# Fused attention and gated feed-forward on one core: value products re-cut by head group, VectorE's score blocks from the first unit into the last

## The chip, the cores and the metric

One core of one Trainium2 chip. The metric is the device time of one execution in microseconds (us), and every kernel is run several times. The profile of one of these executions covers the span from the first to the last instruction, which is about 1.7 us shorter than the time. Beside each run stands the mean clock that TensorE was granted (1.0 is full speed). All runs here are of the same state by the rule used for them (none over 1.5% above the fastest of its kernel), so they are compared as they are; but inside that state time and granted clock move together, and this turns out to matter.

PE is TensorE, PEld its weight loads, DVE is VectorE, ACT is ScalarE, SP is SyncE.

## The reference, cut to what matters

```python
# x: 2048 x 512, 32 heads of 16, F = 1792, all bf16
g = sigmoid((x * gate_w).sum(-1, keepdims=True))
q, k, v = split(x @ wqkv)                       # 32 heads
p = softmax(q @ k.T / 4)                        # per head, 2048 x 2048
a = (p @ v).reshape(S, D) @ wo
b = (silu(x @ w_gate) * (x @ w_up)) @ w_down
return g * a + (1 - g) * b
```

The costly part is the exponential: 32 heads of 2048 x 2048 scores. In the kernel before, ScalarE takes them from TensorE's accumulators in 882 instructions (821.9 us busy) and VectorE in 284 evictions of a block (195.2 us).

## The kernel before

The work is cut into 32 units: four heads (a "group") times one quarter of the queries. The first four units take group 0 for the four quarters; the others follow quarter by quarter. A unit has 16 key tiles times 4 heads: 64 score blocks of 128 x 512. A planner at build time decides, block by block, who takes the exponential.

ScalarE takes blocks in pairs, VectorE takes four blocks as one group with a polynomial in three 16-bit passes each of two kinds:

```python
def emit_pair(bs):                     # ScalarE: two blocks, one instruction
    s_t = ps_s.tile([P, 2 * QBW], F32, tag="s", name="s_t")
    ...                                # two score matmuls into s_t
    act(out=e_t[:], in_=s_t[:], func=ACT.Exp, scale=inv_sqrt_dh)

def emit_d(b):                         # VectorE: one block into the one bank "d"
    d_t = ps_d.tile([P, QBW], F32, tag="d", name="d_t")
    score(d_t[:, :], b)
    ...
    # evicts d_t into y; after the fourth block of the group six passes over 2048 elements:
    # z<-y, u<-z, u<-u*u, u<-u*z, y<-y+u, y<-y, and then the group's value products may run
```

Which of the two it is, is decided here. `un` is the unit, `at_` the block in it. A new VectorE group may begin only while `at_` is at most 50 in an ordinary unit, at most 4 in the last, and not at all in unit 0:

```python
def to_vector():
    un, at_ = divmod(nxt, 4 * KT)
    if vcur:
        ...                            # a group already begun is completed
    if not un or at_ > (50 if un < UNITS - 1 else 4) or y_live[0] >= 3 or sum(v[0] for v in vops) > 6:
        return 0
    return 1
```

A VectorE group that comes after its unit's accumulator (`o_ps`) has been closed is late: its value products go into a separate bank `x_ps`, and VectorE then needs two operations, a copy of the closed bank (`of<-o_ps`) and a sum (`osb<-of,x_ps`). A group that is in time needs only one cast (`osb<-o_ps`).

```python
def pv(bs, last):
    extra = un < closed                # the unit's bank is closed: a late group
    if extra:
        o = m_tile("x_ps")
    ...
    if extra:
        def add():
            vec.tensor_tensor(out=(of_of if blocks[un] else osbs)[un][:, :], in0=of_of[un][:, :], in1=o[:, :], op=ALU.add)
```

The head: keys and queries of group 0 are projected, `|k|` is reduced to a bound that is added to the queries, and four key tiles' values for all 32 heads are evicted by ScalarE before the first exponential:

```python
act(out=q0r[:, :], in_=qp0[:, :], func=ACT.Copy)
for i in range(2):
    vec.tensor_reduce(out=kpart0[:, i:i + 1], in_=kp0[i][:, :], axis=AX.X, op=ALU.max, apply_absolute_value=True)
    v_now(i)                           # four 512-column matmuls, one ScalarE eviction
    act(out=kaug[:, 0, i * 2 * QBW:(i + 1) * 2 * QBW], in_=kp0[i][:, :], func=ACT.Identity, ...)
    ...
vec.scalar_tensor_tensor(out=kneg0, ...)
v_now(2)
mm(bp0[:, :], lhsT=kneg0, rhs=aq0[:, :], start=True, stop=True)      # the bound
...
v_now(3)
```

And the end, after the last unit's sum `osb`. First the projection of the unit before (`al`, `a_l`, four matmuls), then the denominators (`dt`), their reciprocals, the normalised heads, the projection again and the stores:

```python
last_mm(0, osbs[un - 1])                              # al, al, a_l, a_l
for tq in range(TQ):
    mm(dt[:, 4 * tq:4 * tq + 4], lhsT=osb[:, tq * P:(tq + 1) * P], rhs=sel_t[:, :], start=True, stop=True)
recip16(rt[:, :], dt[:, 0:4 * TQ])
...
last_mm(1, on_l)
```

## Time and profile before

| | |
|---|---|
| time, median of the three runs known when predicting | 874.49 us (873.94 to 876.53) |
| span of the profiled execution, mean granted clock | 872.4 us, 0.997 |
| exponentials on ScalarE, VectorE groups | 882, 71 |
| first exponential starts, last one ends | 19.27, 863.62 |
| ScalarE idle among the exponentials | 4.8 us |

The three stretches to keep apart are the head (up to the first exponential, 19.27 us), the stream of exponentials (844.35 us), and the tail (from the end of the last exponential to the end of the span, 8.8 us). ScalarE's time in the stream is a count of instructions times 0.92 us (a run of 58 exponentials took 53.47 us), plus its gaps. The lines are shown in the prediction.

### The profile page before, as it was taken

The numbers are of one execution on the slowest core, as the hardware profiler recorded it, in microseconds if no ns is written. First come the engines' busy times: TensorE is split into PE (matmuls) and PEld (weight loads), VectorE is DVE, ScalarE is ACT, GpSimd is POOL, SyncE is SP. The second block draws the span as 40 slices with busy tenths as digits, with TensorE's granted clock in tenths as the row PEclk, the third lists the DMA queues.
The fourth block names the chain that finished last, engine by engine and source line by source line (L and its number), as shares of the span: only waits on it lengthen the run. The fifth ranks groups of instructions, "written<-read, shape, count | busy, mean of one in ns | idle before, by whom it ended". The sixth has DMA issues, their size and how long they took to land.

```text
span 872.4 us, 14196 instructions
## 1 busy us (share of the span) xinstructions
PE 784.8 (90%) x5078; PEld 207.6 (24%) x5168; DVE 786.9 (90%) x1103; ACT 845.4 (97%) x947; POOL 7.1 (1%) x29
## 2 busy tenths in 40 slices
PE   6999999999999899999989888899898989989985
PEld 2222222222222222222222222222222222222221
DVE  6379999999999999999999999999999998999984
ACT  3999999999999999999999999999999999999995
POOL 3000000000000000000000000000000000000000
PEclk9999999999999999999999999999999999999999
DMA  8401121031101112210011121110011121000000
GB/s 208 111 1 28 29 50 38 21 69 28 31 11 26 40 33 73 52 37 11 4 31 31 34 55 45 42 28 4 4 25 36 36 57 48 21 10 4 5 20 24
DMA packets 87535, 31.98 MB, mean 37 GB/s; under 512 B 75120, under 2 KB 87016, under 8 KB 87464
## 3 DMA queue, kind: packets, MB, share of 16 engines
q1 hardware_dynamic: 86408, 30.94, 14.5%
q8 instruction: 40, 0.66, 0.3%
q10 hardware_dynamic: 1056, 0.13, 0.1%
q14 instruction: 31, 0.25, 0.1%
HBM read 20.83 MB, written 2.34 MB: 27 GB/s over the span
## 4 chain that ended last, share of the span: by engine, by line
ACT 42%; PE 34%; DVE 11%; issue 11%; SPq 1%; DMA 0%; ACTq 0%; DVEq 0%
ACT e_t L161 38%; PE s_t L158 13%; PE o_ps L158 7%; DVE y_t L167 5%; PE d_t L158 4%; PE dps L158 3%; ACT th L161 3%; DVE u_t L167 2%; PE gp L158 2%; PE qp L158 1%; PE up L158 1%; SPq L174 1%; PE kp L158 1%; DVE mt L167 1%; PE a_ps L158 1%
## 5 line engine op out<-in xcount | busy, mean ns | idle before, releaser
L161 ACT ACTIVATE e_t<-s_t 128x1024 bf16<-128x1024 f32 x882 | 821.9, 1079 | 4.8 <-PE s_t L158 3.7
L158 PE MATMUL s_t<-qx,kaug 64*128 64x512 bf16 x1656 | 330.1, 384 | 52.8 <-ACT e_t L161 49.5
L167 DVE TENSOR_SCALAR y_t<-d_t 128x512 uint16<-128x512 f32 x284 | 195.2, 687 | 29.7 <-PE d_t L158 26.2
L158 PEld LDWEIGHTS <-kaug 64*128 64x128 bf16 x2048 | 100.0, 93 | 379.4 <-issue 376.3
L158 PE MATMUL o_ps<-e_t,vaug 128*32 128x512 bf16 x1764 | 172.8, 387 | 1.3 <-ACT e_t L161 0.7
L158 PE MATMUL d_t<-qx,kaug 64*128 64x512 bf16 x264 | 99.6, 377 | 0.6 <-DVE y_t L167 0.3
L167 DVE TENSOR_TENSOR y_t<-y_t,u_t 128x2048 uint16<-128x2048 uint16 x71 | 86.6, 1219 | 0.9
L167 DVE TENSOR_TENSOR u_t<-u_t 128x2048 f16<-128x2048 f16 x71 | 86.5, 1218 | 0.8
L167 DVE TENSOR_TENSOR u_t<-u_t,z_t 128x2048 f16<-128x2048 f16 x71 | 86.4, 1217 | 0.4
L158 PEld LDWEIGHTS <-vaug 128*32 128x32 bf16 x2048 | 45.4, 94 | 133.1 <-issue 129.3
L158 PE MATMUL dps<-wd_t,mt 128*128 128x512 bf16 x200 | 62.4, 384 | 3.0 <-issue 3.0
L158 PE MATMUL gp<-xT,wg 128*128 128x512 bf16 x199 | 62.2, 384 | 2.5 <-issue 2.4
L158 PE MATMUL up<-xT,wu 128*128 128x512 bf16 x207 | 62.2, 383 | 2.0 <-issue 1.9
L167 DVE TENSOR_SCALAR y_t<-y_t 128x2048 uint16<-128x2048 uint16 x71 | 48.9, 688 | 1.2
L167 DVE TENSOR_SCALAR u_t<-z_t 128x2048 f16<-128x2048 uint16 x71 | 48.7, 687 | 0.7
L167 DVE TENSOR_SCALAR z_t<-y_t 128x2048 uint16<-128x2048 uint16 x71 | 48.6, 684 | 0.1
L167 DVE SCALAR_TENSOR_TENSOR gs<-th,gp 128x512 bf16<-128x512 bf16 x56 | 38.2, 681 | 4.2 <-ACT th L161 3.7
L167 DVE SCALAR_TENSOR_TENSOR mt<-gs,up 128x512 bf16<-128x512 bf16 x56 | 38.1, 681 | 2.2
L161 ACT ACTIVATE th<-gp 128x512 bf16<-128x512 f32 x56 | 36.4, 650 | 0.0
L158 PEld LDWEIGHTS <-mt 128*128 128x128 bf16 x263 | 16.2, 99 | 42.8 <-issue 36.5
L158 PE MATMUL s_t<-on,kaug 64*128 64x512 bf16 x108 | 21.7, 383 | 3.6 <-ACT e_t L161 3.1
L158 PEld LDWEIGHTS <-wu 128*128 128x128 bf16 x224 | 13.7, 97 | 32.0 <-issue 27.6
(101 smaller groups left out, 347.1 us busy)
## 6 DMA issues: line engine op xcount, KB each, us to landing
wg<-in_B_w_gate_dram SPq DMA_DIRECT2D x56, 128.0 KB
wu<-in_B_w_up_dram SPq DMA_DIRECT2D x56, 128.0 KB
on<-osb SPq DMA_DIRECT2D x120, 16.0 KB
rb<-rr SPq DMA_DIRECT2D x15, 128.0 KB
wd_t<-in_B_w_down_dram SPq DMA_DIRECT2D x1, 1792.0 KB
qx<-qst SPq DMA_DIRECT2D x112, 16.0 KB
out_dram<-o_t SPq DMA_DIRECT2D x12, 128.0 KB
kaug<-on SPq DMA_DIRECT2D x20, 64.0 KB
```

The lines of the kernel that those rows point to most:

```text
L158: ordered(nc.tensor.matmul(*args, **kw))
L161: ordered(nc.scalar.activation(*args, **kw))
L167: return lambda *a, **kw: ordered(f(*a, **kw))
L174: nc.sync.dma_start_transpose(out=xT[:, dc, :], in_=x[:, dc * P:(dc + 1) * P])
```

## The change

The intent is to give VectorE work where it had little: score blocks from the ninth block of unit 0 on, and groups begun up to block 24 of the last unit. To make room for the former, the values are re-cut. Group 0's 64 columns are made first, for four key tiles at a time (sixteen 64-column matmuls and one 256-column eviction); the other 448 columns are made later, spread over the next units. The core of it, with cuts:

```diff
+    nc.scalar.dma_start(out=wv[:, :, 0:64], in_=A_wqkv[:, 2 * D:2 * D + 64]...)
-    nc.sync.dma_start(out=wv, in_=A_wqkv[:, 2 * D:3 * D]...)
+    nc.sync.dma_start(out=wv[:, :, 64:D], in_=A_wqkv[:, 2 * D + 64:3 * D]...)
 ...
+    def v0_pieces(t0, act_evac=False):      # 4 key tiles, group 0 only: 16 matmuls of 64 columns, 1 eviction
+    ...
-                    mm(st["p"][:, 0:D], lhsT=xT[:, dc, tt * P:(tt + 1) * P], rhs=wv[:, dc, :], ...)
+                    mm(st["p"][:, 64:D], lhsT=xT[:, dc, tt * P:(tt + 1) * P], rhs=wv[:, dc, 64:D], ...)
 ...
-        v_now(i)                            # and v_now(2), v_now(3): four full tiles in the head
+        if i == 0:
+            for _, f, _ in v0_pieces(0, act_evac=True):
+                f()
 ...                                         # three small VectorE operations moved behind the first scores
+    for i in range(1, KT // 4):
+        v_chain[i] = pace.add(v0_pieces(4 * i), 0, 4 * i + 1)
+    v_rest = [pace.add(v_pieces(tt), 2, int(12 + 3 * tt)) for tt in range(KT)]
 ...
-    f0, f1 = 44, SLOTS - 8                  # the feed-forward's start in the plan
+    f0, f1 = 72, SLOTS - 8
 ...
-        if not un or at_ > (50 if un < UNITS - 1 else 4) or y_live[0] >= 3 or sum(v[0] for v in vops) > 6:
+        if nxt < 8 or at_ > (50 if un < UNITS - 1 else 24) or y_live[0] >= 3 or sum(v[0] for v in vops) > 6:
```

> **What bounds the kernel now.** I read the page first (busy shares, then the chain that ended last), then the groups of instructions, then the busy time by stretches of one unit each, and last the timelines of the first 20 us and the last 40 us.
>
> ```profile
> PE 784.8 (90%) x5078; PEld 207.6 (24%) x5168; DVE 786.9 (90%) x1103; ACT 845.4 (97%) x947; POOL 7.1 (1%) x29
> ...
> ACT 42%; PE 34%; DVE 11%; issue 11%; SPq 1%; DMA 0%; ACTq 0%; DVEq 0%
> ...
> L161 ACT ACTIVATE e_t<-s_t 128x1024 bf16<-128x1024 f32 x882 | 821.9, 1079 | 4.8 <-PE s_t L158 3.7
> L158 PE MATMUL s_t<-qx,kaug 64*128 64x512 bf16 x1656 | 330.1, 384 | 52.8 <-ACT e_t L161 49.5
> L167 DVE TENSOR_SCALAR y_t<-d_t 128x512 uint16<-128x512 f32 x284 | 195.2, 687 | 29.7 <-PE d_t L158 26.2
> L167 DVE TENSOR_TENSOR u_t<-u_t 128x2048 f16<-128x2048 f16 x71 | 86.5, 1218 | 0.8
> L167 DVE TENSOR_SCALAR u_t<-z_t 128x2048 f16<-128x2048 uint16 x71 | 48.7, 687 | 0.7
> ```
>
> ScalarE is the bound. Its 882 exponentials, each over a pair of score blocks, idle only 4.8 us in all, while the score matmuls wait 49.5 us for them to free a bank. The remaining 284 of the 2048 blocks are VectorE's: four evictions and six long passes make a group of four.
>
> ```profile
> 0.00:27.20 27.20, 19.22 (x85) 6.36 (x87) 15.94 (x44) 13.73 (x17) 7.07 (x29) 1.00 0.93 237
> 27.26:54.50 27.24, 25.49 (x153) 6.67 (x155) 12.44 (x20) 27.10 (x31) 0.00 (x0) 1.00 0.11 20
> 54.52:81.80 27.28, 25.52 (x165) 6.40 (x167) 26.19 (x38) 26.80 (x31) 0.00 (x0) 1.00 0.11 22
> ...
> 845.06:872.30 27.24, 16.88 (x120) 5.20 (x120) 13.92 (x24) 17.58 (x19) 0.00 (x0) 0.89 0.06 20
> ```
>
> The columns are PE, PEld, DVE, ACT and POOL busy. VectorE is near full in the middle (26.19 of 27.28), but half idle in the second and the last stretch, where it has few or no score blocks. Those two holes are what the change is after. Outside the exponentials lie a head of 19.27 us and a tail of 8.8 us:
>
> ```profile
> 13.60 0.60 ACT L161 ACTIVATE q0r<-qp 128x512 bf16<-128x512 f32 x1 [10.51 <-PE qp L158]
> 14.29 2.75 PE L158 MATMUL vp<-rb,xT 128*128 128x512 bf16 x12 [0.73 <-DMA rb<-in_A_wqkv_dram]
> 15.35 0.60 ACT L161 ACTIVATE vaug<-vp 128x512 bf16<-128x512 f32 x1 [1.16 <-PE vp L158]
> 17.30 1.41 DVE L167 SCALAR_TENSOR_TENSOR qx<-bp,vsel,qx 128x512 bf16<-128x512 f32 x2 [0.50 <-PE bp L158]
> 18.31 1.10 ACT L161 ACTIVATE vaug<-vp 128x512 bf16<-128x512 f32 x2
> 18.45 0.71 PE L158 MATMUL s_t<-qx,kaug 64*128 64x512 bf16 x4
> ...
> 840.72 0.37 PE L158 MATMUL d_t<-qx,kaug 64*128 64x512 bf16 x1
> ...
> 848.77 14.85 ACT L161 ACTIVATE e_t<-s_t 128x1024 bf16<-128x1024 f32 x16 [0.98 <-PE s_t L158]
> ...
> 864.11 0.69 DVE L167 CAST osb<-o_ps 128x512 bf16<-128x512 f32 x1 [5.34 <-PE o_ps L158]
> ```
>
> Head: four value evictions sit on ScalarE ahead of the first exponential, behind a matmul run that waits for the value weights. Tail: the last exponential ends at 863.62 and VectorE has then been idle for 5.34 us, so only the last bank's copy and 7.6 us of normalising, projecting and storing follow.
>
> [...] the trace's loads of that kind average 97. So a 64-column matmul behind its own 128-column load costs about 0.1 us, not an eighth of a 512-column one. [...] the timeline of before shows its instructions in program order.
>
> **The change part by part.**
> (1) Score blocks. The instruction lists of the two built programs have 882 and 878 exponentials, 284 and 292 VectorE evictions. By unit of 64 blocks, unit 0 goes from 0 to 8 VectorE blocks and the last unit from 4 to 8; the middle gives back 4. A run of 58 exponentials took 53.47 us, a run of 65 took 60.20 us, so one more costs 0.92. Four fewer: -3.7 us on the bound engine.
>
> (2) Head. ScalarE's four evictions become one. The first value product needs 64 weight columns, loaded early, and 16 narrow matmuls (16 x 0.1 = 1.6 us from 13.5), so it is done by about 15.2 and nothing waits on the big weight load. The key evictions follow the reductions: 14.3 to 15.4 and, after the second maximum at 15.8, 15.9 to 17.0. The query chain becomes the limit. Three small VectorE operations leave it, and the bound matmul no longer queues behind twelve value matmuls (it sat at 16.88 though its operand was ready at 16.27). The two scaled adds start near 16.85 instead of 17.30; the first pair's scores need only the first add (0.7 us), so the first exponential starts at about 18.1 instead of 19.27: -1.15 us. [...]
>
> (3) Value products. The remaining 12 key tiles of group 0 come in threes of sixteen narrow matmuls, 4.8 us of PE against twelve full tiles before; the other 28 heads (16 tiles of four 448-column matmuls, 12 us) move into the next units. PE waits 49.5 us for ScalarE in all, so this lies beside it. VectorE copies go from 12 x 0.69 to 16 x 0.63 + 3 x 0.4: +3 us, spread over units with room.
>
> (4) Tail. The list of before has 22 pairs of scores after the last VectorE score matmul, the changed one only 10. Call that matmul's start T. In before, T is 840.72 and the last exponential ends at 863.62: 22.9 us, less the 0.98 gap 21.9 = 22 x 0.92 + 1.7. In the changed kernel the last exponential ends at T + 10 x 0.92 + 1.7 = T + 10.9. VectorE, in order, has after its last eviction (done near T + 1.3): one normalisation (0.36), three passes and three passes of two groups (tensor_scalar at 0.6 to 0.7 from start to start, tensor_tensor at 1.13 to 1.25) and four output projections' adds at 0.67. By start-to-start intervals that is 13.5 us: T + 14.8. One add, the third, must wait for a projection matmul that PE issues only behind the last value products, at about T + 10.2 instead of 9.2: T + 15.8. Then the last bank is copied and the late group added, two operations instead of one: 1.3 us, T + 17.1; then the same 7.6 us. The end is at T + 24.7, which is 13.8 us after the last exponential instead of 8.8: **+5.0 us**.
>
> (5) The 0.98 us gap at 848.77, where PE held the scores back behind a projection that waited for VectorE's normalisations, should vanish, because in the changed list they precede the projection by several pairs: -0.9.
>
> Sum: -3.7 - 1.15 + 5.0 - 0.9 = -0.75. From 874.49 that is **873.7 us**.
>
> **The rivals.**
> A. The tail is free: VectorE catches up in the last unit and the exponentials still end last. Then -3.7 - 1.15 - 0.9: 868.7 us. For it: VectorE idles 5.34 us at the end of before, and whoever chose 24 instead of 4 as the last unit's limit presumably saw a use. Against it: the list puts a late group's product after the last bank's close, as a separate product with an add, so the kernel's own plan has the group late; and counting its operations by the rows above, VectorE gets some 30 us of work in a last unit of 25.7 us of exponentials, where before had 20.
> B. VectorE becomes the bound in unit 0 or in the units with the 28-head copies, so score matmuls for it wait and hold ScalarE back. Unit 0 gets an estimated 26 us of VectorE work in 25.7 us. Each group late by a microsecond would show as gaps of the size of the 0.98; three or four make 877 us. Against it: before runs whole units at 31 us of VectorE work per 24 us (12 blocks) by borrowing from the next, with a total ScalarE gap of 4.8.
> C. The head is not shortened, because the last input transpose, which PE waits for at 12.32, lands later behind the added load, or because the narrow matmuls crowd the first score pairs (twelve of them stand between the second and third pair: 1.2 us against 0.9 of an exponential). Then +0.5 to +1.2 on my sum: 874.5 to 875.
>
> **Range and chances.** The firm terms are the pairs (-3.7) and the sign of the head. The tail is the wide one: +5 with perhaps 2 either way, since it sums twenty intervals; the gaps in the middle can move by 1.5 either way with a wholly re-ordered list. Together about 3 us, with A the more likely side: 869.5 to 877.0. Two per cent is 17.5 us, more than every term added with one sign, so within 2% has 0.98, faster 0.01, slower 0.01.
>
> **What would show it.** The count of exponentials is 878. The first starts near 18.1 (between 17.9 and 18.6). The distance from the last exponential's end to the span's end is near 13.8 instead of 8.8, with VectorE busy without a gap through it and the last copy of the bank behind a late pass. ScalarE's gaps among exponentials stay under 6 us in all. Step 4 is wrong if that distance stays under 10; step 2 if the first exponential is after 19; the idea of ScalarE as the bound is wrong if its gaps grow beyond 8 us, most of all in unit 0. I would be wrong in total if the tail is hidden (rival A) or if a stall of several microseconds lies in the units that take the 28-head copies.

Where the text is marked as cut, times that were not read from a trace, a remark on VectorE's queue and a guess at the cost of 64 KB more in the head are left out. No term of the sum is among them: it stays -3.7 - 1.15 + 5.0 - 0.9 = -0.75, so 873.7 us. What is left of the cut paragraph speaks of TensorE's 128-column weight loads (97 ns) and of VectorE's instructions, which the tail takes in the order of the program.

Some lengths in parts 2 and 3 and in rival B are the author's estimates, for shapes and stretches that before's trace does not hold: 0.1 us for a narrow matmul (from the 97 ns), 12 us for the 64 matmuls of 448 columns, 0.63 and 0.4 us for VectorE's copies of 448 and 256 columns, and 26 us of VectorE work in unit 0. For comparison: in before's line above, twelve 512-column value matmuls took 2.75 us. In after, sixteen narrow matmuls took 0.63 us, the 64 matmuls of 448 columns were 17.7 us of PE's busy time, VectorE's copies took 0.62 and 0.42 us, and VectorE was busy for 19.57 of the first 25.67 us of the stream.

## The result, and the profile after

The changed kernel took 875.78 us (median of four runs, 874.76 to 876.12), the kernel before in the same rounds 875.32 (four runs, 873.94 to 876.53). The ratio is 1.0004, with a 95% interval from 0.9984 to 1.0023: the same. A ratio is the mean time of one kernel's runs over that of the other's of the same rounds, so not quite the ratio of the medians that are quoted.

The profiled execution has a span of 874.4 us at a mean granted clock of 0.987. First its page: the chain that ended last, and two groups of instructions (after the bar: busy us, mean ns of one; after the second bar: idle before them, and what ended it).

```profile
PE 46%; ACT 36%; issue 8%; DVE 8%; DMA 1%; SPq 1%; DVEq 0%; ACTq 0%
...
L161 ACT ACTIVATE e_t<-s_t 128x1024 bf16<-128x1024 f32 x878 | 818.3, 1092 | 5.8 <-PE s_t L158 4.7
L158 PE MATMUL s_t<-qx,kaug 64*128 64x512 bf16 x1644 | 329.9, 386 | 45.7 <-ACT e_t L161 42.9
```

The exponentials are 878, as planned, and the score matmuls still wait for ScalarE 43 us in all: ScalarE is still the bound of the stream. Its 5.8 us of idle time include 1.12 us before the first exponential, which belong to the head. Among the exponentials it idles 4.7 us, against 4.8 in before. Read by the three stretches:

| us | before | after | difference |
|---|---|---|---|
| head: start of the first exponential | 19.27 | 18.53 | -0.74 |
| stream: to the end of the last one | 844.35 | 840.23 | -4.12 |
| tail: from there to the end of the span | 8.8 | 15.6 | +6.9 |
| span | 872.4 | 874.4 | +2.0 |

The last column adds up to the 2.0 us by which these two profiled executions differ. The medians of the runs differ by less, 0.46 us.

**Head and first exponentials.** This is the timeline after (start, duration, engine, operation; in brackets the idle time before it and what ended it).

```profile
12.87 1.02 PE L158 MATMUL kp<-xT,mt 128*128 128x512 bf16 x4 [0.47 <-DMA xT<-in_A_x_dram]
13.95 0.63 PE L158 MATMUL vp<-rb,xT 128*128 128x64 bf16 x16
...
16.86 0.39 PE L158 MATMUL bp<-aq,mt 128*128 128x512 bf16 x1 [2.29 <-DVE mt L167]
...
18.10 0.39 PE L158 MATMUL s_t<-qx,kaug 64*128 64x512 bf16 x2 [0.84 <-DVE qx L167]
18.53 1.99 ACT L161 ACTIVATE e_t<-s_t 128x1024 bf16<-128x1024 f32 x2 [1.12 <-PE s_t L158]
20.79 2.85 ACT L161 ACTIVATE e_t<-s_t 128x1024 bf16<-128x1024 f32 x3 [0.27 <-PE s_t L158]
23.80 1.02 ACT L161 ACTIVATE e_t<-s_t 128x1024 bf16<-128x1024 f32 x1 [0.16 <-PE s_t L158]
25.33 52.39 ACT L161 ACTIVATE e_t<-s_t 128x1024 bf16<-128x1024 f32 x57 [0.50 <-PE s_t L158]
```

Three things stand in it. The first exponential no longer waits behind ScalarE's own evictions; it waits 1.12 us for the scores. The last input transpose is used at 12.87, where before had 12.32. And PE now has nothing to do for 2.29 us before the bound matmul and for 0.84 us before the first scores, where before filled this time with value products. What follows from that shows in the windows (columns: us, busy PE, PEld, DVE, ACT, POOL, then the granted clock, the DMA share and GB/s), first of after:

```profile
20.00:22.00 2.00, 2.00 (x15) 0.65 (x12) 0.36 (x1) 1.73 (x3) 0.00 (x0) 0.50 0.37 97
22.00:24.00 2.00, 2.00 (x13) 0.53 (x15) 1.28 (x3) 1.84 (x3) 0.00 (x0) 0.50 1.01 342
```

and of before:

```profile
20.00:22.00 2.00, 1.58 (x8) 0.56 (x8) 0.69 (x1) 2.00 (x4) 0.00 (x0) 1.00 0.59 141
```

The clock is 0.50 in after and 1.00 in before. At half the clock PE is full (2.00 of 2.00 us in both windows) and cannot feed ScalarE: the gaps of 0.27, 0.16 and 0.50 us end at 20.79, 23.80 and 25.33, and the clock is at 0.50 from 18.5 to 25.3. They are gaps in unit 0, but VectorE (busy 0.36 of 2 us) is not what PE waits for.

**Tail.** The timeline of after, from the last exponentials and the third of the four output projections' adds:

```profile
854.99 3.77 ACT L161 ACTIVATE e_t<-s_t 128x1024 bf16<-128x1024 f32 x4
...
858.27 0.75 DVE L167 SCALAR_TENSOR_TENSOR kaug<-a_ps,gval,bblk 128x512 f32<-128x512 f32 x1 [0.97 <-PE a_ps L158]
...
863.99 0.62 PE L158 MATMUL x_ps<-y_t,vaug 128*32 128x512 bf16 x4 [4.78 <-DVE y_t L167]
864.54 1.03 PE L158 MATMUL al<-wo_l,osb 128*128 128x512 bf16 x2
864.66 0.69 DVE L167 TENSOR_TENSOR osb<-of,x_ps 128x512 bf16<-128x512 f32 x1
866.55 0.26 DVE L167 RECIPROCAL rt<-dt 128x16 bf16<-128x16 f32 x1 [1.21 <-PE dt L158]
...
870.28 1.40 DVE L167 SCALAR_TENSOR_TENSOR mt<-a_l,gval,kaug 128x512 bf16<-128x512 f32 x2
```

In before, the last two of these were

```profile
865.15 0.26 DVE L167 RECIPROCAL rt<-dt 128x16 bf16<-128x16 f32 x1 [0.36 <-PE dt L158]
...
868.24 1.40 DVE L167 SCALAR_TENSOR_TENSOR mt<-a_l,gval,kaug 128x512 bf16<-128x512 f32 x2
```

In after the last exponential ends at 858.76, but VectorE still works through the last group; its value products run at 863.99, and the sum ends at 865.35. PE has then stood idle for 4.78 us, and its clock has fallen, as the windows show:

```profile
860.00:862.00 2.00, 0.00 (x0) 0.00 (x0) 1.97 (x4) 0.00 (x0) 0.00 (x0) 0.90 0.00 0
862.00:864.00 2.00, 0.01 (x2) 0.01 (x2) 1.97 (x3) 0.00 (x0) 0.00 (x0) 0.50 0.00 0
```

It fell at 861.6, when PE had been idle for 2.4 us, and stays at 0.50 to the end (before had 1.00 in 864 to 868). And the four projection matmuls `al`, `a_l`, which in before ran while VectorE cast the bank, now stand between `x_ps` and the denominators at half speed: the reciprocal waits 1.21 us for them instead of 0.36.

### The profile page after: what moved, and what is told of

The parts are those of the page before. It is cut to its first block, busy times and chain, and to the rows that moved or that the text cites. A ratio compares the mean times of both kernels' runs of the same rounds, so it can differ in the third digit from the quotient of the medians.

```text
span 874.4 us, 14435 instructions
## 1 busy us (share of the span) xinstructions
PE 804.5 (92%) x5232; PEld 210.0 (24%) x5232; DVE 807.5 (92%) x1134; ACT 839.9 (96%) x940; POOL 7.4 (1%) x30
## 4 chain that ended last, share of the span: by engine, by line
PE 46%; ACT 36%; issue 8%; DVE 8%; DMA 1%; SPq 1%; DVEq 0%; ACTq 0%
ACT e_t L161 33%; PE s_t L158 17%; PE o_ps L158 8%; PE d_t L158 5%; PE dps L158 4%; PE gp L158 4%; DVE y_t L167 3%; ACT th L161 3%; PE up L158 2%; DVE u_t L167 2%; PE qp L158 1%; PE vp L158 1%; PE a_ps L158 1%; PE kp L158 1%; PE x_ps L158 1%
## 5 line engine op out<-in xcount | busy, mean ns | idle before, releaser
L167 DVE TENSOR_SCALAR y_t<-d_t 128x512 uint16<-128x512 f32 x292 | 200.5, 687 | 33.4 <-PE d_t L158 30.5
L158 PE MATMUL d_t<-qx,kaug 64*128 64x512 bf16 x276 | 104.9, 380 | 0.3 <-DVE y_t L167 0.3
L167 DVE TENSOR_TENSOR u_t<-u_t 128x2048 f16<-128x2048 f16 x73 | 88.9, 1218 | 0.9
L167 DVE TENSOR_TENSOR y_t<-y_t,u_t 128x2048 uint16<-128x2048 uint16 x73 | 88.9, 1218 | 0.7
L167 DVE TENSOR_TENSOR u_t<-u_t,z_t 128x2048 f16<-128x2048 f16 x73 | 88.8, 1217 | 0.4
L158 PE MATMUL dps<-wd_t,mt 128*128 128x512 bf16 x224 | 67.8, 384 | 0.0
L158 PE MATMUL gp<-xT,wg 128*128 128x512 bf16 x224 | 67.8, 384 | 0.0
L158 PE MATMUL up<-xT,wu 128*128 128x512 bf16 x224 | 65.2, 383 | 0.0
L158 PE MATMUL vp<-rb,xT 128*128 128x448 bf16 (+1 forms) x128 | 22.0, 284 | 0.0
```

Of the source, the lines that this page charges most:

```text
L158: ordered(nc.tensor.matmul(*args, **kw))
L167: return lambda *a, **kw: ordered(f(*a, **kw))
```

## The experiments

Twelve kernels were run, five rounds each, all with a correct result. The reasons that they were to tell apart:

- **The tail theory** (the first): the last unit's late VectorE group takes back what the fewer exponentials gain. Its rival: the tail is a feature of the profiled execution, or the time goes elsewhere.
- **The clock theory**: the halved clock behind PE's idle stretches costs time, in the head (gaps among the exponentials) and in the tail (slow last matmuls). Its rivals: VectorE's new blocks in unit 0 cause the gaps; or only the order of the last matmuls counts.
- **The load theory** (the third): the added early load of the narrow value weights delays the input transposes. Its rival: their landing varies by itself.

All of them at a glance; each ratio is against the kernel before in the same rounds, whose median was 875.68 (runs 1 to 4), 875.78 (5 to 8) and 877.15 (9 to 12).

| run | median us (lowest to highest) | ratio [95%] |
|---|---|---|
| 1 last_unit_4 | 872.54 (869.33 to 877.39) | 0.9967 [0.9940, 0.9995] |
| 2 tail_order | 876.13 (874.67 to 879.27) | 1.0011 [0.9991, 1.0031] |
| 3 tail_warm | 876.54 (873.78 to 878.39) | 1.0016 [0.9996, 1.0036] |
| 4 head_warm | 874.77 (873.38 to 877.98) | 0.9996 [0.9975, 1.0017] |
| 5 before_unit0 | 874.01 (873.47 to 876.83) | 0.9983 [0.9965, 1.0000] |
| 6 before_last24 | 877.50 (877.03 to 879.86) | 1.0028 [1.0010, 1.0047] |
| 7 head_narrow_later | 875.10 (873.98 to 876.17) | 0.9995 [0.9977, 1.0013] |
| 8 short_tail_warm_head | 867.99 (866.39 to 869.21) | 0.9912 [0.9894, 0.9931] |
| 9 last4_warm | 869.49 (869.32 to 871.99) | 0.9924 [0.9904, 0.9944] |
| 10 last4_later | 871.56 (870.02 to 873.64) | 0.9940 [0.9920, 0.9960] |
| 11 last4_fill_more | 869.48 (869.20 to 871.04) | 0.9918 [0.9899, 0.9938] |
| 12 values_only | 876.85 (875.08 to 877.42) | 0.9996 [0.9977, 1.0015] |

### 1. last_unit_4: the last unit's limit back at 4

```diff
-        if nxt < 8 or at_ > (50 if un < UNITS - 1 else 24) or ...
+        if nxt < 8 or at_ > (50 if un < UNITS - 1 else 4) or ...
```

> The changed kernel with the last unit's limit back from 24 to 4, so VectorE takes 4 score blocks there instead of 8; the instruction lists are the same up to that unit, with 880 exponentials instead of 878. Theory 1 (the late VectorE group in the last unit costs about 6.9 us of tail: 15.6 us from the last exponential to the end instead of 8.8): the distance goes back to 8.8, two more exponentials cost 1.85, so about 5.0 us shorter than the changed kernel, near 870.8 us, ratio to before about 0.995. Rival (the tail is not the cause; the time is lost in the gaps of unit 0 and the middle): two exponentials more and no gain, 1.8 us longer, near 877.6.

Its profiled execution has 880 exponentials, the last ends at 859.89, and the span is 868.6: a tail of 8.7 us, like that of before. The last cast and the last adds in it:

```profile
860.37 0.69 DVE L167 CAST osb<-o_ps 128x512 bf16<-128x512 f32 x1 [1.68 <-PE o_ps L158]
...
864.51 1.40 DVE L167 SCALAR_TENSOR_TENSOR mt<-a_l,gval,kaug 128x512 bf16<-128x512 f32 x2
```

VectorE is idle again before the cast, and no late group is summed. Two more exponentials (+1.84) against 6.9 us of tail make -5.0; the ratios (0.9967 against 1.0004 in other rounds) give some 3 us of it. The six runs spread over 8 us, and the slower ones have the lower mean clock (877.39 at 0.982, 869.33 at 0.995), which may hide part of the effect; this is not shown. The tail theory holds.

### 2 and 3. tail_order and tail_warm: the last projection earlier, without and with filling

Both are the changed kernel, with the two `al` matmuls issued before the late group's `x_ps`; tail_warm repeats them (22 in all), so that PE has work while it waits for VectorE. The repeats compute the same product into the same bank.

```diff
         extra = un < closed
+        if extra and un == UNITS - 1 and nxt == nb and not early:
+            early.append(ps_s.tile([P, 2 * QBW], F32, tag="s", name="al"))
+            for k in range(1):                     # tail_warm: range(11)
+                for tq in range(2):
+                    mm(early[0][:, tq * QBW:tq * QBW + D], lhsT=osbs[un - 1][:, tq * P:(tq + 1) * P], rhs=wo_l[:, 0, :], start=True, stop=...)
```

> The changed kernel with two of the four last-unit projections that do not depend on the late group issued on PE before its product instead of after. Theory 1b (of the 9.05 us between the last bank's sum and the end, against 7.6 before, part is that these four matmuls now stand between the sum and the softmax denominators): about 0.8 us shorter than the changed kernel. Rival (all of the excess is the halved clock): under 0.3 us.

> As the run with two projections issued early, with 20 further repeats of them that fill PE's idle 4.8 us while it waits for VectorE's late passes; results unchanged. Theory 1c (the granted clock halves because PE idles there, and the final matmuls run at 600 instead of 380 ns): the clock stays 1.0 to the end, the sum of the last bank to the end takes 7.2 to 7.6 us instead of 9.05, in all about 1.6 us shorter than the changed kernel. Rival (the clock falls for another reason, or the final matmuls are not on the path): no better than the run without the repeats.

The last two `a_l` matmuls took 0.63 us each in after and 0.38 in before. The trace of tail_warm shows what filling does. One window of it, then the sum and the last adds:

```profile
862.00:864.00 2.00, 1.75 (x11) 0.51 (x9) 1.86 (x4) 0.00 (x0) 0.00 (x0) 1.00 0.00 0
```

```profile
863.67 0.69 DVE L167 TENSOR_TENSOR osb<-of,x_ps 128x512 bf16<-128x512 f32 x1
...
867.99 1.40 DVE L167 SCALAR_TENSOR_TENSOR mt<-a_l,gval,kaug 128x512 bf16<-128x512 f32 x2
```

The clock is 1.00 where after had 0.50, and from the end of the sum (864.36) to the end of the span (872.1) it is 7.7 us instead of 9.05: the 7.6 that the prediction used. In tail_order, with the order changed and the clock at 0.50 from 868.2 on, the same stretch is 8.5 us. So, in these traces, the order is worth 0.5 us of the 1.35 and the clock the other 0.8. The tail of tail_warm is 14.3 us, that of tail_order 15.1, that of after 15.6. But neither shows a gain in time: both medians are 0.4 to 0.8 us above that of after. The stream's gaps differ by more than these 1.3 us; in the profiled execution of tail_order the clock was at 0.50 in every window from 22 to 34 us, with 7.3 us of gaps among the exponentials. So the tail's 1.3 us is shown in traces alone.

### 4. head_warm: PE kept busy before the bound matmul

```diff
     bp0 = ps_d.tile([P, QBW], F32, tag="d", name="bp0")
+    for _ in range(10):
+        mm(bp0[:, :], lhsT=wpad[0][:, 0, :], rhs=xT[:, 0, 0:QBW], start=True, stop=True)
     mm(bp0[:, :], lhsT=kneg0, rhs=aq0[:, :], start=True, stop=True)
```

The ten products are thrown away, since the bound matmul starts the bank anew.

> The changed kernel with 10 idle matmuls into the bank of the query bound, in PE's 2.3 us of waiting in the head (14.6 to 16.9). Theory 2 (PE's idle head halves the granted clock from 18.7 to about 25 us, and the slow score matmuls open gaps of 0.27, 0.16 and 0.50 us before exponentials): the clock stays 1.0 there, these gaps vanish, 0.7 to 1.0 us shorter than the changed kernel; the first exponential is not later. Rival (the gaps come from the twelve narrow matmuls and the added VectorE score blocks crowding PE): clock up, gaps stay, under 0.3 us.

One window and the first run of exponentials in its profile:

```profile
20.00:22.00 2.00, 1.40 (x11) 0.45 (x9) 0.59 (x1) 2.00 (x3) 0.00 (x0) 1.00 0.70 181
```

```profile
18.79 117.08 ACT L161 ACTIVATE e_t<-s_t 128x1024 bf16<-128x1024 f32 x127 [1.12 <-PE s_t L158]
```

The clock is 1.00, and 127 exponentials follow one another without a listed gap, with VectorE's blocks of unit 0 still in place. That answers the rival: the gaps of after in unit 0 come from the halved clock, not from VectorE. The other traces agree. All four with the filling (runs 4, 8, 9 and 11) have the clock at 1.00 in the head and no gap in unit 0; the other seven with the re-cut values have both the dip and gaps, run 12 among them, which has no VectorE blocks there. In time it is about 1 us by the medians (874.77 against 875.78), which these runs do not resolve: the intervals overlap.

### 5. before_unit0: only the permission for unit 0, in the kernel before

```diff
-        if not un or at_ > (50 if un < UNITS - 1 else 4) or ...
+        if nxt < 8 or at_ > (50 if un < UNITS - 1 else 4) or ...
```

> The kernel before with one condition changed: VectorE may take score blocks from unit 0 on; values, head and the last unit's limit of 4 stay. 878 exponentials instead of 882, and 21 pairs of scores after VectorE's last score matmul. Theory (the four pairs are worth 3.7 us where the tail stays clear): tail 8.8, about 3.7 us shorter than before, near 871.5. Rival (unit 0 of before is full of 512-column value products, an estimated 28 us of PE per 29 of exponentials, so the added scores open gaps): ScalarE's gaps grow by 2 us or more and the gain is under 2 us.

In before's profile PE was busy for 27.59 of the 29.44 us from 19.27 on, which is the expectation's 28 of 29. The run has 878 exponentials, four fewer than before, and a tail of 8.7 us; the gain by count would be 3.7. By the ratio it is 1.5 us. ScalarE's gaps are 7.4 us in its profile instead of 4.8, so 1.1 of the 3.7 are left; the new ones lie behind unit 0's blocks, in unit 1, at full clock (1.00 in all windows from 48 to 68 us), and the head was late in this execution:

```profile
15.94 4.42 PE L158 MATMUL vp<-rb,xT 128*128 128x512 bf16 x12 [2.06 <-DMA rb<-in_A_wqkv_dram]
...
52.17 5.61 ACT L161 ACTIVATE e_t<-s_t 128x1024 bf16<-128x1024 f32 x6 [1.07 <-PE s_t L158]
```

So the rival keeps something here: with the old order of the values, the blocks of unit 0 are partly paid for with gaps that the clock doesn't explain. PE's timeline shows what stands before them. Ahead of the 1.07 us gap PE ran six 512-column value matmuls in a row (1.47 us from 49.64); ahead of the 0.76 us gap it waited 0.79 us for VectorE's copy of a value tile. No run removes either. The first line also shows a second kind of head: the big value load landed at 15.94 instead of 14.29 (16.51 in run 6), PE waited 2.06 us for it, the clock was at 0.50 from 16.8 to about 20.3, and the first exponential began at 21.98. This head has the same instructions as that of before, up to the first exponentials. Before's profile, which the prediction was built on, was therefore of an early one.

### 6. before_last24: only the limit 24, in the kernel before

```diff
-        if not un or at_ > (50 if un < UNITS - 1 else 4) or ...
+        if not un or at_ > (50 if un < UNITS - 1 else 24) or ...
```

> The kernel before with the last unit's limit at 24 instead of 4: 880 exponentials, 12 pairs of scores after VectorE's last score matmul, the last group's product after the last bank's close. Theory 1 (the late group costs the tail): two pairs fewer, -1.85; from the last exponential to the end 12.5 to 14.5 us instead of 8.8, so 2 to 4 us longer than before, near 878. Rival (the tail of the changed kernel is long for another reason, say the values' spread): tail under 10 us and 1 to 2 us shorter than before.

Slower by 0.28%, 2.5 us, with an interval that excludes 1. Its tail:

```profile
867.71 0.62 PE L158 MATMUL x_ps<-y_t,vaug 128*32 128x512 bf16 x4 [2.31 <-DVE y_t L167]
868.38 0.69 DVE L167 TENSOR_TENSOR osb<-of,x_ps 128x512 bf16<-128x512 f32 x1
870.27 0.26 DVE L167 RECIPROCAL rt<-dt 128x16 bf16<-128x16 f32 x1 [1.21 <-PE dt L158]
```

The last exponential ends at 864.96 and the span is 878.1, so the tail is 13.1 us, 4.4 more than before's; two exponentials fewer (880) give back 1.84; the difference is 2.5, which is what the ratio shows (the medians differ by 1.7). The pattern is that of after, down to the 1.21 us. Here the clock fell at 866.7, 1.3 us into a wait of 2.31 us, and was at 0.50 from then on. The tail theory holds on the other kernel too.

### 7. head_narrow_later: the narrow value load behind the transposes

```diff
-    nc.scalar.dma_start(out=wv[:, :, 0:64], ...)
+    nc.sync.dma_start(out=wv[:, :, 0:64], ...)
```

> The changed kernel with the narrow 64-column value load issued from SyncE's queue after the input transposes, instead of from ScalarE's queue before them. Theory 3 (the extra early 64 KB delayed the second weight slice from 5.05 to 5.41 and the last transpose's landing from 12.32 to 12.87): both go back, the first exponential is at about 18.0 instead of 18.5, 0.5 us shorter, which is at the edge of what the times can show. Rival (the delay is chance between executions): the last transpose still lands at 12.6 to 13.1; or the value products now wait for the load and the first exponential is no earlier.

In its profile the last transpose is used at 12.44 and the first exponential starts at 18.10, which is what the theory asks for. But the kernels of runs 8 and 10, with the same order of loads, had 13.01 and 13.06. Over the fourteen profiled executions, this transpose was used between 12.32 (before) and 13.27 (last_unit_4), in both orders. What holds is the chain behind it: 5.66 us from this transpose to the first exponential in after, in this run and in runs 1, 4, 8, 9, 11 and 12, and 5.87 in runs 2, 3 and 10. The load theory isn't shown; the landing varies from execution to execution, and too few were profiled to tell a shift of half a microsecond.

### 8 to 11. The limit 4 with filling, and its parts

Run 8 puts the edits of runs 1, 4 and 7 together. Run 9 leaves out run 7's, run 10 leaves out run 4's, run 11 is run 9 with three more filling matmuls behind the bound matmul, into a bank not yet in use:

```diff
     mm(bp0[:, :], lhsT=kneg0, rhs=aq0[:, :], start=True, stop=True)
+    idle = ps_o.tile([P, QBW], F32, tag="o", name="idle")
+    for _ in range(3):
+        mm(idle[:, :], lhsT=wpad[0][:, 0, :], rhs=xT[:, 0, 0:QBW], start=True, stop=True)
```

> The three edits together on the changed kernel: the last unit's limit at 4, the narrow load after the transposes, and ten filling matmuls in PE's wait in the head. If the theories add: 5.0 + 0.5 + 0.9 us shorter than the changed kernel, near 869.5 us, ratio to before 0.992 to 0.995, faster than both kernels; tail 8.8, gaps among exponentials under 4 us, the clock 1.0 from 18 to 26 us. If the clock's dips come at random however PE is filled, the times spread over 5 us as with the limit alone and the median is near 872.

> The changed kernel with the last unit's limit at 4 and the ten filling matmuls in the head, the narrow load left where the change put it. The three edits together gave 867.99 us, the limit alone 872.54. Theory 2 (the filling matmuls keep the clock up and so close the gaps of unit 0): near 868.0 to 868.8, clocks of 0.994 or more in every run, spread under 4 us. Rival (the later narrow load did it): near 872, clocks down to 0.98 again.

> The changed kernel with the last unit's limit at 4 and the narrow load issued after the transposes, without filling matmuls. Theory 2: as the limit alone, near 871.5 to 872.5, with the clock's dip after 18 us in the trace. Rival (the later load brings the gain of the three edits): near 868.

> The limit at 4, and ten filling matmuls before the query bound plus three more behind it, in PE's second wait of 0.84 us. If the clock still dips in some runs with ten, three more help: 0 to 1 us better than with ten, spread smaller. If ten are enough: the same within 0.5 us. If they stand in the way of the first scores: 0.2 to 0.5 us longer.

Run 8 is the fastest of the study: 867.99 us, 0.9912 of before. Its exponentials, and its last cast:

```profile
L161 ACT ACTIVATE e_t<-s_t 128x1024 bf16<-128x1024 f32 x880 | 818.6, 1096 | 3.0 <-PE s_t L158 2.6
```

```profile
856.70 0.69 DVE L167 CAST osb<-o_ps 128x512 bf16<-128x512 f32 x1 [1.68 <-PE o_ps L158]
```

Its gaps among the exponentials are 1.9 us (3.0 with the 1.12 of the head), the tail is 8.7 us, and the six runs' clocks lie between 0.995 and 0.998. Without filling (run 10) the clocks are 0.986 to 0.991, the clock was 0.50 from 18 to 34 us in its profile, the gaps are 7.1 us by the same count, and it took 871.56. Filling with the narrow load early (run 9) took 869.49, with one of its six runs at a clock of 0.990, below the 0.994 that was expected of all; three more matmuls (run 11) changed nothing, 869.48. Put as two by two, with the early narrow load:

| median us | limit 24 | limit 4 |
|---|---|---|
| no filling | 875.78 (after) | 872.54 (run 1) |
| filling | 874.77 (run 4) | 869.49 (run 9) |

The limit is worth 3.2 and 5.3 us, filling 1.0 and 3.1. These are medians of different rounds, in which before moved from 875.3 to 877.2, so a microsecond in the differences is uncertain. By ratios, filling is worth 0.43% at limit 4 (0.9924 against 0.9967) and 0.28% beside the later load (0.9912 against 0.9940).

### 12. values_only: the re-cut values without either permission

```diff
-        if nxt < 8 or at_ > (50 if un < UNITS - 1 else 24) or ...
+        if not un or at_ > (50 if un < UNITS - 1 else 4) or ...
```

> The changed kernel without its two permissions to VectorE: no score blocks in unit 0, and the last unit's limit at 4. What stays is the other values' order, the narrow load and the later start of the second block. 884 exponentials, two more than before, clear tail. By the trace of before whose first exponential is at 19.27: +1.85 - 0.7 = 1.1 us longer than before. But in two executions of kernels with the head of before, the big value load landed late and the first exponential came at 22.0 and 22.6: if that is usual, the head gains 2 to 3 us on the median and this kernel is 0.5 to 1.5 us shorter than before, near 874.7.

The same time as before (0.9996). It has 884 exponentials, and its head is 0.66 us shorter than before's (18.61), but it has two exponentials more (+1.84) and 6.8 us of gaps among them instead of 4.8. So the re-cut alone saves nothing. Only 0.56 us of these gaps lie in the head's dip of the clock (0.50 in the windows from 20 to 26 us) or just after it; the others come from 81 us on, so the emptied head is the smaller part. Together with unit 0's blocks (run 1) the re-cut gives 0.9967, and the limit 24 takes that back.

### Time and clock over the runs

Taking each of the 76 runs of the changed kernel and the twelve against the mean of its own kernel, a mean clock lower by 0.01 goes with a time longer by 5.6 us (correlation -0.91). That this is cause and not only company is shown for the head by the filling (runs 8 to 11); for single runs without a profile it is not known where in the execution their clock was low.

The profiled executions show something that no run was made for: the clock also falls in the middle of the stream. In before it did so in the last unit:

```profile
846.00:848.00 2.00, 1.66 (x7) 0.35 (x7) 1.50 (x3) 1.78 (x2) 0.00 (x0) 0.51 0.00 0
```

It was at 0.50 from 846.0 to 849.4, around before's gap of 0.98 us at 848.77, and none of PE's listed waits in the 3.4 us before it was longer than 0.53 us. After has such a dip from 769.4 to 772.9, with gaps of 0.48 and 0.70 us in it and just after it.

In each of these two traces the clock changes only at instants that lie whole multiples of 3.41 us apart: before's dip in the last unit lasts 3.41 us, after's two dips before the tail 6.83 and 3.41. In the 3.41 us before their five falls PE was busy for 54% of the time (before, 846.0), 23% (before, 869.9), 23% (after, 18.5), 58% (after, 769.4) and 30% (after, 861.6). A share that decides can't be read from this: before had 56% from 863.1 to 866.5, and its clock stayed at 1.00 behind it. Nor did every long wait bring a fall: in run 2's tail PE waited 4.23 us, and the clock was 1.00 in all windows from 860 to 868. This is a reading of these traces after the fact; no run varied the share in steps. Where the instants lie differs between the two executions. That the same kernel meets a dip in one execution and misses it in another may follow, but is not shown: each kernel was profiled once.

## Why the prediction was right or wrong

**In total** it was right: 873.7 predicted, 875.78 measured, inside 869.5 to 877.0, and within 2%. The expected gain of the fewer exponentials went to the tail, as step 4 said. The sign of the small difference was not told: 0.75 us shorter was predicted, and the profiled executions differ by 2.0 us the other way, the medians by 0.46, which is within noise. The halved clock stands in no step.

**Step 1, score blocks (-3.7): right.** There are 878 exponentials. The stream is 4.12 us shorter: 3.7 by the count and some 0.3 by the gaps that the timelines list, 3.6 us in after against 3.9 in before; the small rest was not traced. Before's 0.98 us gap is gone, but after has 0.93 early in unit 0 and 1.18 at 771 to 773.

**Step 2, the head (-1.15): the sign right, the size 0.74.** The failed term is "the two scaled adds start near 16.85 instead of 17.30". They started at 17.29, because all inputs came 0.55 us later (the last transpose 12.87 instead of 12.32). From that transpose on it went as predicted, or a little better: 5.66 us, which from 12.32 would have been 17.98. So this part of rival C happened in the profiled execution. Its cause, the added load, isn't shown: the landing varies, and that of the one profile before was the earliest of fourteen. The other half of rival C, crowding by the narrow matmuls, fell: sixteen of them took 0.63 us, not 1.6, and gaps between the first pairs came with the halved clock and went with the filling. (Rival C's own sum is slightly off: 0.5 to 1.2 on 873.7 is 874.2 to 874.9.)

**Step 3, values beside PE's slack: right about the sum, but blind to a side.** There was room for them. Moving four full tiles of value products out of the head, however, left PE idle for 2.29 and 0.84 us just before the stream, and the clock was at 0.50 for the next 6.8 us. The prediction did not ask what the emptied head would do to it. This cost 0.93 us of gaps in the profiled execution, and 3 us or more in others (run 10).

**Step 4, the tail (+5.0): the sign and the mechanism right, the size +6.9.** Let T be the start of the last VectorE score matmul, at 848.01. The last exponential ended at T + 10.75 (predicted 10.9). The third add was held up by a projection until T + 10.26 (10.2). The sum ended at T + 17.34 (17.1). The failed term is "then the same 7.6 us": it was 9.05. Two things were in it that the prediction took over from before unexamined: PE would come from a long wait, at half the clock, and the four `al`, `a_l` matmuls, which before hid behind the cast, would stand ahead of the denominators. With the order changed (run 2) the stretch was 8.5, with order and clock both changed (run 3) 7.7. The rest of the +1.9 is the sum's 0.24 and the 0.15 at the last exponential (the tail is a difference of the two), with the roundings.

**Step 5, the 0.98 us gap (-0.9): right for the profiled execution, but by luck.** No such gap lies in after's last unit. The reason given, a projection that waits for VectorE's normalisations, is not what the traces show. Run 7 has after's instructions there, and a gap of 0.98 us at 848.11; its page puts the mean clock of the slice from 828.6 to 850.4 below 0.90, where after's windows from 840 to 860 show 1.00. In before PE waited only 0.34 us for VectorE ahead of the projection, and that in the dip (0.50 from 846.0 to 849.4). The stretch of before that the prediction shows has a mean clock of 0.89, which it did not follow up.

**Rival A** (a free tail, 868.7) fell in its premise, yet its number is not far from what limit 4 gives (run 1: 869.33 at best, a median of 872.54), since there the tail really is free at the price of two exponentials. **Rival B** (VectorE the bound in unit 0) fell for the changed kernel (run 4), while in the old order of values something of its size appeared (run 5): one of the three new gaps follows a wait for VectorE's value copy, another a row of value products on PE.

**Still open:** whether PE's share of work alone brings the clock's dips in the middle of the stream, and what they cost on the average; whether the early narrow load delays the transposes at all; how much the order and the clock in the tail are worth in time, which no median showed; and why the value load lands at 14.3 us in before's profile and at 15.9 and 16.5 in those of two kernels with the same head (runs 5 and 6).

## What to carry to other kernels

Work moved to an idle engine in the last stage must be counted to the end of its own chain: this group's passes outlived the last exponential, and cost more than the two exponentials that it saved. When work is taken out of a stretch where an engine waits, ask what the wait does to TensorE's clock and to the work behind it (here, behind waits of 2.29 and 0.84 us, 6.8 us at 0.50); ten matmuls thrown away ahead of the first scores went with 1 to 3 us here. And profile more than one execution before resting half a microsecond on a landing time, or on a single gap: look at the clock around the gap first.
